# Linear attention and SwiGLU in one kernel: six of twelve token groups in natural order as four blocks of 64, decay over whole groups, one plain causal mask

## The chip, the cores and the metric

The kernel runs on one core of one Trainium2 chip. The metric is the device time of one execution in microseconds (us). All times below are of this case's runs. Each run of an experiment was timed on the same chip and in the same call as the kernel before, in alternation.

## The reference

Four sequences of 768 tokens with eight heads of 64 columns go through causal linear attention with a decay per head, in blocks of 64 tokens. The result (3072 x 512) goes through a SwiGLU FFN of width 1536.

```python
for b in range(nb):                       # blocks of 64 tokens
    intra = einsum('bhic,bhjc->bhij', qb, kb) * Dmask      # lam^(i-j), i >= j
    intra = einsum('bhij,bhjd->bhid', intra, vb)
    inter = einsum('bhid,bhde->bhie', qb * lam_pow, kv_state)
    out[:, :, sl] = intra + inter
    kv_state = lam**64 * kv_state + einsum('bhsd,bhse->bhde', kb * rev_pow, vb)
...
y = (silu(x @ w_gate) * (x @ w_val)) @ w_out               # x: attention, 3072 x 512
```

## The kernel before

Attention is done in 12 groups of 256 tokens of one sequence, FFN in 6 tiles of 512 tokens (two groups). TensorE does FFN products all the time, and the visits to attention are put between them by hand. A load gives each partition a pair of neighbouring tokens, so a row is 2 x 64 floats, 512 bytes, and k, q and v of a group are one transfer each.

```python
const = tile_pool("const", bufs=1); wpool = ...            # on-chip memory is handed out in this order
raw_pool = tile_pool("raw", bufs=10)                       # k, q, weights as loaded (f32)
...
def load_fp32(g, eng, src, what, h0=0, h1=H):              # 128 partitions x 8 heads x 512 B
    eng.dma_start(out=st[(what, g)][:, h0:h1], in_=gsrc(src, g, h0)[:, 0:h1 - h0])
...
mask = const.tile([128, 2, HP, 2, BLK], BF16, name="mask") # causal times a decay per head: 4096 B per partition
...
def scores(g, ...):                                        # 32 products of 128 columns into 4 banks
    ...
def inter(g, first):                                       # state times q: 8 full products, 128 columns
    ...
def intra(g, first):                                       # masked scores times v: 32 products of 128 columns
    ...
def attend(g):
    core(g)                                                # inter, intra, eviction
    if g + 1 < NG:
        ahead(g + 1)                                       # state update, scores of the next group
...
at(s1b[6], ahead, 4)
for _ in range(4):
    at(s1b[6], wo_cast)                                    # output weight casts on GpSimd
at(s1b[6], v_scale, 5, nc.gpsimd)
at(s1b[10], core, 4)
at(s1b[11], ffn_out, 0, 0)
at(s1b[11], ahead, 5)
```

The eight PSUM banks go round in a ring. GpSimd keeps the running state, scales v and casts weights; ScalarE evicts and casts k; VectorE masks and casts q. One queue (SP) issues the loads and the transposes, in the order of the program.

## Time and profile before

| | before |
|---|---|
| time, median of 3 | 231.78 us (231.72 to 231.91) |
| span of the profiled execution | 230.1 us |
| TensorE busy | 220.4 us, 96% |
| 512 B packets, 4 to 36 us, median | 27 ns |
| a later attention visit, inter to FFN | 1.81 us |

The chain of waits, the timelines and the hole at 68 us are shown and read in the prediction. In a timeline, a line gives the start in us, the length in us, the engine, the line of the kernel, the operation, the tile written and the tiles read, and in square brackets the engine's idle time before it and what ended that. "PEld" is the loading of weights, "SPq" and "ACTq" are issues of transfers. The packet durations come from the trace's packet records.

### The profile page before, as it was taken

What the parts mean: (1) busy time and instruction counts of PE and PEld (TensorE: products, weight loads), DVE (VectorE), ACT (ScalarE), POOL (GpSimd) and SP (SyncE); (2) the same over time, 40 slices, a digit from 0 to 9 for tenths busy, and PEclk for the clock granted to TensorE, in tenths of its full rate; (3) what the DMA queues carried; (4) which work ended last, traced back from release to release, by engine and by line L of the source; (5) the groups of instructions that cost most, each with busy time, mean ns of one, the idle gap of its engine ahead of it and who ended that gap; (6) DMA issues with size and microseconds to landing.
All of it is one profiled execution on the core that took longest, in us unless ns stands there. A gap on an engine that the chain in (4) does not pass through costs nothing.

```text
span 230.1 us, 5416 instructions
## 1 busy us (share of the span) xinstructions
PE 220.4 (96%) x2224; PEld 121.4 (53%) x2236; DVE 102.2 (44%) x187; ACT 105.1 (46%) x203; POOL 79.8 (35%) x113
## 2 busy tenths in 40 slices
PE   7899999999987999999999999999999999999994
PEld 3565456888854544464544544544544544444443
DVE  5763968675915014747273273273261223132200
ACT  6978585755532535363344363354343233322321
POOL 4476857743997703829050050050020000000000
PEclk9999999999999999999999999999999999999999
DMA  6999999899996278395918806905101101101122
GB/s 196 346 360 382 363 346 303 195 266 361 339 224 219 91 184 276 96 313 128 282 56 202 257 3 160 296 3 137 46 3 46 48 0 47 46 3 46 46 91 91
DMA packets 68906, 39.66 MB, mean 172 GB/s; under 512 B 20114, under 2 KB 64402, under 8 KB 68882
## 3 DMA queue, kind: packets, MB, share of 16 engines
q1 hardware_dynamic: 64370, 32.64, 49.6%
q10 hardware_dynamic: 4512, 6.69, 8.0%
q8 instruction: 17, 0.28, 0.5%
q14 instruction: 7, 0.06, 0.1%
HBM read 28.31 MB, written 6.29 MB: 150 GB/s over the span
## 4 chain that ended last, share of the span: by engine, by line
PE 78%; POOL 7%; DMA 6%; SPq 3%; ACT 2%; issue 2%; DVE 1%; POOLq 0%; DVEq 0%; ACTq 0%
PE bank L460 25%; PE bank L438 23%; PE bank L445 23%; DMA woraw<-in_moe_w_out_dram 3%; POOL wo_sb L212 3%; DMA qraw<-in_q_dram 2%; PE bank L401 2%; SPq L92 2%; PE bank L308 2%; PE bank L386 2%; PE bank L338 1%; POOL kvl L376 1%; POOL kvz L374 1%; POOL kvf L370 1%; POOL wv_sb L201 1%
## 5 line engine op out<-in xcount | busy, mean ns | idle before, releaser
L448 DVE TENSOR_TENSOR h<-sil,bank 128x512 bf16<-128x512 bf16 (+1 forms) x87 | 50.9, 592 | 102.5 <-PE bank L445 91.5
L438 PE MATMUL bank<-xt,wg_sb 128*128 128x512 bf16 (+1 forms) x348 | 76.6, 343 | 0.1
L445 PE MATMUL bank<-xt,wv_sb 128*128 128x512 bf16 (+1 forms) x348 | 76.5, 342 | 0.2 <-POOL wv_sb L201 0.2
L442 ACT ACTIVATE sil<-bank 128x512 bf16<-128x512 f32 (+1 forms) x87 | 45.5, 525 | 46.9 <-PE bank L438 44.5
L460 PE MATMUL bank<-wo_sb,h 128*128 128x512 bf16 (+1 forms) x288 | 64.9, 370 | 1.5 <-POOL wo_sb L212 0.8
L445 PEld LDWEIGHTS <-wv_sb 128*128 128x128 bf16 x348 | 33.9, 98 | 28.9 <-POOL wv_sb L201 1.1
L438 PEld LDWEIGHTS <-wg_sb 128*128 128x128 bf16 x348 | 32.8, 98 | 27.7 <-DVE xt L412 0.3
L460 PEld LDWEIGHTS <-h 128*128 128x128 bf16 x300 | 29.2, 98 | 33.8 <-issue 1.6
L462 ACT COPY osb<-bank 128x512 f32<-128x512 f32 (+1 forms) x24 | 13.8, 576 | 57.3 <-PE bank L460 52.5
L370 POOL TENSOR_TENSOR kvf<-kvl,ups 128x256 f32<-128x256 f32 x16 | 12.5, 782 | 64.5 <-ACT ups L360 62.9
L315 DVE TENSOR_TENSOR ssb<-bank,mask 128x512 bf16<-128x512 f32 x40 | 26.0, 683 | 8.6 <-PE bank L308 8.4
L218 POOL TENSOR_TENSOR v_s<-v,rev 128x1024 bf16<-128x1024 f32 (+1 forms) x14 | 23.1, 1655 | 8.3 <-DMA v<-in_v_dram 4.9
L412 ACT CAST xt<-bank 128x512 bf16<-128x512 f32 x21 | 14.3, 740 | 9.3 <-PE bank L401 8.3
L374 POOL CAST kvz<-kvf 64x256 bf16<-64x256 f32 x32 | 13.5, 421 | 1.7
L308 PE MATMUL bank<-qkt 64*64 64x128 bf16 x384 | 9.0, 219 | 1.2 <-DVE qkt L280 0.8
L240 DVE TENSOR_TENSOR qk<-qraw,qd 128x1024 bf16<-128x1024 f32 x8 | 10.2, 1269 | 0.0
L238 ACT CAST qk<-kraw 128x1024 bf16<-128x1024 f32 x9 | 9.4, 1042 | 0.0
L376 POOL TENSOR_TENSOR kvl<-kvf,lamblk 128x256 f32<-128x256 f32 x12 | 8.2, 683 | 1.0
L201 POOL CAST wv_sb<-wraw 128x1024 bf16<-128x1024 f32 (+1 forms) x7 | 6.5, 934 | 5.4 <-DMA wraw<-in_moe_w_val_dram 5.2
L401 PE MATMUL bank<-ssb,v_s 64*64 64x128 bf16 x384 | 8.1, 219 | 0.2 <-DVE ssb L315 0.2
L308 PEld LDWEIGHTS <-qkt 64*64 64x64 bf16 x384 | 6.6, 106 | 3.0 <-ACT qkt L272 1.8
L212 POOL CAST wo_sb<-woraw 128x1024 bf16<-128x1024 f32 x6 | 6.6, 1131 | 3.9 <-DMA woraw<-in_moe_w_out_dram 3.9
(57 smaller groups left out, 100.3 us busy)
## 6 DMA issues: line engine op xcount, KB each, us to landing
out_dram<-osb ACTq DMA_DIRECT2D x23, 256.0 KB, 2.0
kraw<-in_k_dram SPq DMA_DIRECT2D x10, 512.0 KB, 5.2
qraw<-in_q_dram SPq DMA_DIRECT2D x10, 512.0 KB, 6.2
v<-in_v_dram SPq DMA_DIRECT2D x10, 512.0 KB, 6.5
woraw<-in_moe_w_out_dram SPq DMA_DIRECT2D x6, 512.0 KB, 7.2
wraw<-in_moe_w_gate_dram SPq DMA_DIRECT2D x5, 512.0 KB, 7.0
wraw<-in_moe_w_val_dram SPq DMA_DIRECT2D x5, 512.0 KB, 7.0
kraw<-in_k_dram SPq DMA_DIRECT2D x4, 256.0 KB, 4.4
```

What stands on the lines that cost most here:

```text
L218: eng.tensor_tensor(out=st[("vs", g)][:, h0:h1], in0=st[("v", g)][:, h0:h1].rearrange("p h (s d) -> p h s d", s=2), in1=bap(rev, [[2, h1 - ...
L308: nc.tensor.matmul(sp[(c, h2)][b2 * M:b2 * M + M, n:n + BLK], tt[dp, 0, s, hp, b2 * M:b2 * M + M], tt[dp, 1, :, hp, b2 * M:b2 * M + M], st ...
L315: nc.vector.tensor_tensor(out=ssb[:, h2, 2 * c:2 * c + 2].rearrange("p a s n -> p a (s n)"), in0=sp[(c, h2)].rearrange("p (a x) -> p a x", ...
L370: nc.gpsimd.tensor_tensor(out=kv, in0=kvl[b], in1=u, op=ALU.add)
L374: nc.gpsimd.tensor_copy(out=kvz[b][(i + 1) % 2 if r else 2][dp, :, h2, :], in_=kv[dp])
L412: fns[r](out=xt[:, g % 2, :, r].rearrange("p h (m s) -> p h s m", s=2), in_=op[r].rearrange("p (h s m) -> p h s m", h=HP, s=2))
L438: nc.tensor.matmul(gp[:, 0:N], wg_sb[:, mc, fs], xt[:, b0 // 2:b1 // 2, mc].rearrange("p g b n -> p g (b n)"), start=(mc == 0), stop=(mc = ...
L442: nc.scalar.activation(sil[:, 0:N], gp[:, 0:N], AF.Silu)
L445: nc.tensor.matmul(vp[:, 0:N], wv_sb[:, mc, fs], xt[:, b0 // 2:b1 // 2, mc].rearrange("p g b n -> p g (b n)"), start=(mc == 0), stop=(mc = ...
L448: nc.vector.tensor_tensor(out=h_sb[:, fc, b0:b1].rearrange("p b n -> p (b n)"), in0=sil[:, 0:N], in1=vp[:, 0:N], op=ALU.mult)
L460: nc.tensor.matmul(ps, h_sb[:, fc, b], wo_sb[:, fc, c0:c1], start=(fc == 0), stop=(fc == FC - 1))
L462: fn(out=osb[:, c0:c1], in_=ps)
```

## The change

The intent is to take TensorE time out of the attention visits: with four blocks of 64 tokens instead of two of 128, every small product has 64 columns instead of 128. A block of 64 tokens needs tokens in natural order, one per partition, so rows are 64 floats, 256 bytes. To keep all four quadrants of the array at work, the upper 64 partitions hold head pairs exchanged; the transfers do this. The decay inside a group moves into the scales of q and v, so one causal mask serves all heads and GpSimd's state work shrinks.

```diff
+    NAT0 = 6                                   # groups 6 to 11 in natural order
...
+        if what == "v":
+            parts = [(0, 128, 0, 1, 0, H)]
+        else:
+            parts = [(0, M, 0, 1, 0, H)] + [(M, M, h2, 2, 1 - h2, HP) for h2 in range(2)]
+        for s in range(2):
+            for p0, n, d0, dh, s0_, nh in parts:
+                eng.dma_start(out=t[p0:p0 + n, ...], in_=...)   # k 6, q 6, v 2 per group
...
-    irow = const.tile([128, 2, M], FP32, name="irow")
-    irev = const.tile([128, 2], FP32, name="irev")
-    ifwd = const.tile([128, 2], FP32, name="ifwd")
-    (cinv, rev, qd, lamblk, qdec, cinvt)
-    mask = const.tile([128, 2, HP, 2, BLK], BF16, name="mask")
+    irow = const.tile([128, 2, 2, M], FP32, name="irow")
+    ipos = const.tile([128, 8], FP32, name="ipos")
+    causaln = const.tile([128, M], BF16, name="causaln")
+    (dec, qdn, lamgrp, a qdec of twice the size, two guards)
...
+    def scores_n(g):                           # 32 products of 64 columns, 2 banks
+    def guard(g):                              # one column copied by ScalarE between inter and intra
+        nc.scalar.copy(out=t, in_=st[("op", g)][1][:, 511:512])
...
     def attend(g):
-        core(g)
-        if g + 1 < NG:
-            ahead(g + 1)
+        core_a(g)                              # inter, guard
+        if g + 1 < NG:
+            upd_mm(g + 1); upd_copy(g + 1); scores(g + 1)
+        core_b(g)                              # intra, eviction
+        if g + 1 < NG:
+            state(g + 1)
...
-    for _ in range(4):
-        at(s1b[6], wo_cast)
+    at(s1b[6], wo_cast)
+    at(s1b[6], wo_cast)
     at(s1b[6], v_scale, 5, nc.gpsimd)
-    at(s1b[10], core, 4)
+    at(s1b[8], wo_cast, ACTC)                  # the fifth cast on ScalarE
+    at(s1b[8], wo_cast)
+    at(s1b[9], core_a, 4)
+    at(s1b[10], core_b, 4)
```

## The prediction

> **What bounds the kernel now.** I read the page's busy shares and the chain that ended last first, to see whether one engine sets the time.
>
> ```profile
> PE 220.4 (96%) x2224; PEld 121.4 (53%) x2236; DVE 102.2 (44%) x187; ACT 105.1 (46%) x203; POOL 79.8 (35%) x113
> ...
> PE 78%; POOL 7%; DMA 6%; SPq 3%; ACT 2%; issue 2%; DVE 1%; POOLq 0%; DVEq 0%; ACTq 0%
> ```
>
> TensorE is busy 96% of 230.1 us and carries 78% of the chain; GpSimd and DMA carry 13%. So only two things count: TensorE time in the attention blocks, and the few holes where GpSimd or DMA makes TensorE wait. The FFN (lines 438, 445, 460) isn't changed: its 864 full-width products (288 + 288 + 288 in units of 512 columns) at 0.216 us (0.86 us for four, in the chain) are 186 us.
>
> Then the timeline of TensorE, for a steady stage. Columns: start, length in us, engine, line, operation, count.
>
> ```profile
> 97.97 1.03 PE L445 MATMUL bank<-xt,wv_sb 128*128 128x512 bf16 x4
> 98.84 0.61 PE L386 MATMUL bank<-qkt,kvz 128*128 128x128 bf16 x8
> 99.38 0.64 PE L401 MATMUL bank<-ssb,v_s 64*64 64x128 bf16 x32
> 99.85 0.45 PE L338 MATMUL bank<-v_s,qk 64*64 64x64 bf16 x32
> 100.12 0.65 PE L308 MATMUL bank<-qkt 64*64 64x128 bf16 x32
> 100.84 1.02 PE L438 MATMUL bank<-xt,wg_sb 128*128 128x512 bf16 x4
> ```
>
> Ends are modelled, so I use starts. One attention visit is inter (386, the state applied to q), intra (401), the state update (338) and the next group's scores (308), with FFN work touching on both sides. 32 small products with 64 moving columns (338) take 99.85 to 100.12, **0.27 us**; 32 with 128 columns (401) take 0.47 us. That difference is what the change can earn. The later visits, without a wait, last 1.81 us (112.92 to 114.73, and three more alike).
>
> Last, the holes: the same timeline around 68 us, and GpSimd's.
>
> ```profile
> 65.69 1.98 PE L460 MATMUL bank<-wo_sb,h 128*128 128x512 bf16 x7
> 68.06 0.59 PE L460 MATMUL bank<-wo_sb,h 128*128 128x512 bf16 x2 [0.39 <-POOL wo_sb L212]
> 69.05 0.59 PE L460 MATMUL bank<-wo_sb,h 128*128 128x512 bf16 x2 [0.39 <-POOL wo_sb L212]
> 70.91 0.45 PE L338 MATMUL bank<-v_s,qk 64*64 64x64 bf16 x32 [1.27 <-POOL v_s L218]
> ```
>
> ```profile
> 65.01 3.98 POOL L212 CAST wo_sb<-woraw 128x1024 bf16<-128x1024 f32 x4
> 68.96 1.90 POOL L218 TENSOR_TENSOR v_s<-v,rev 128x1024 bf16<-128x1024 f32 x1
> ```
>
> The first output block is 12 products, 2.59 us from 65.69, so the update could begin at 68.37 after a change of tiling; it begins at 70.91. **2.5 us** are lost to GpSimd, which does four weight casts and only then scales v.
>
> **What the Trainium skill says.** "TensorE: Matmul & The Clock Gate", part 1 (Wait — 56ns, not 53.3ns?) gives N ÷ 2.4 GHz + about 2.5 ns per warm matmul, and part 3 says that products in different tiles of the array overlap. The trace agrees: 0.216 us for 512 columns; four quadrants at 128 columns would give 8 x 56 ns = 0.45 us for 32, and 0.47 is seen. With 64 columns the rule would give 0.23 and 0.27 is seen; I use 0.27. "TensorEngine Tiling (Array Packing)", Key Properties, says that changing the tiling mode drains the engine. The trace: FFN products that should end at 88.41 are followed by the update at 88.50, so about 0.09 us a change. The same page, Gotcha 1, says that different row tiles can't access one PSUM bank simultaneously. That explains the new guard: with exchanged head pairs inter and intra of one quadrant come from different row halves. "DMA: Bandwidth & Descriptors", Specifications, puts line rate at 512 B and over. No load of this kernel has 256 B rows, but its transposes move 256 B packets: in the trace's packet records they take 18 ns (median) against 27 ns for 512 B, that is 1.33 times the time per byte.
>
> **The change, part by part.**
>
> 1. Groups 6 to 11, TensorE. With four blocks of 64 tokens, scores and intra keep 32 products but with 64 columns, and inter becomes 32 products of 64 x 64 in four quadrants in place of 8 full ones. Each of the three should take the update's 0.27 us. Inter 0.54 less the change of tiling in it = 0.45, to 0.27: -0.18. Intra 0.47 to 0.27: -0.20. Scores, 88.78 to 89.33 less 0.09 = 0.46, to 0.27: -0.19. The update stays: the last groups go from 16 products in two quadrants (about 0.26, worked out from 113.93 to 114.73) to 24. Tiling changes per visit stay two. So -0.57 for each of five visits, -0.19 for group 6's early scores: **-3.0**. The wait for the eviction at 100.84 (0.16 us) should go too, since two score banks less are taken: -0.16.
>
> 2. The guard, a one-column ScalarE copy between inter and intra. Inter's issue 0.27 + a product's own length 0.19 + 0.09 to wake ScalarE (the update ends at 59.82, its copy starts at 59.91) + 0.16 for a tiny activation + 0.09 back = 0.80 us from inter's start. In five visits the update and scores (0.27 + 0.27) stand between, so intra is reached at 0.81: nothing lost. The last visit, group 11, has nothing between: 0.27 + 0.53 wait + 0.27 + two changes 0.18 = 1.25 against 1.11 (182.35 to 183.46): **+0.15**.
>
> 3. The hole at 68 us. One cast goes to ScalarE, and scaling v of group 5 comes before the last. GpSimd: the state of group 4 shrinks from 4.7 us (60.36 to 65.0) to 0.75 + 0.42 + 0.75 + 0.61 + 0.42 = about 3.0, end 63.4; two casts to 65.4, v scaled by 67.3, last cast 68.3. But ScalarE's cast needs the fifth piece of the weight, whose last packet plus the 1.65 us that the first piece took to release GpSimd gives 64.0; ScalarE, being in order, is done at 65.0 and only then does a silu (0.38) and the guard of group 4, so intra of group 4 goes at 65.65 in place of 64.23. After it: intra 0.47, one FFN column block 0.86, output block 2.59, changes 0.18: update of group 5 at about 69.8, not 70.91, **-1.1**. From there to the third tile's FFN the old time is 9.73 us (80.64); two more changes of tiling, less the 0.23 us gap before 78.27, make it about 9.8: **+0.1**.
>
> 4. Start and groups 2 and 3. Zero fills (12 x 0.27 us) and mask tables (2.9 us) leave VectorE, scaled q/k copies become one (0.84 to 0.59), the first states drop from 2.9 to 1.8 us on GpSimd. But DMA is saturated up to 36 us (345 to 385 GB/s in the windows), and v of group 2 isn't scaled before 36.6, so TensorE can't run far ahead. Group 2 loses its 0.32 us wait and gets an exposed guard of about 0.45; groups 3 and 4 get two more changes each. I call it **0**.
>
> 5. Loads of the last six groups: 14 transfers of 256 B rows per group in place of 3. Spacing of issues at the start is 0.54 us, so 7.6 us of issue; data 6144 packets / 16 x 18 ns = 6.9 us. The tightest group is 8:
>
> ```profile
> 95.16 1.55 SPq L231 DMA_TRANSPOSE qkt<-qk  x1
> 96.76 0.57 SPq L92 DMA_DIRECT2D kraw<-in_k_dram  x1
> 97.38 0.86 SPq L92 DMA_DIRECT2D qraw<-in_q_dram  x1
> 98.29 1.35 SPq L92 DMA_DIRECT2D v<-in_v_dram  x1
> 106.03 2.36 SPq L231 DMA_TRANSPOSE qkt<-qk  x1
> ```
>
> On these clocks q would land at 96.1 + 12 x 0.54 + 2 = 104.6, VectorE wants it at about 104, the transpose goes at about 106 as before and takes 4.4 us, and its reader comes at 114. It is hidden, with about 3 us to spare. **0**.
>
> Sum: -3.0 - 0.16 + 0.15 - 1.1 + 0.1 = -4.0. 231.78 - 4.0 = 227.8 us; I say 227.7, 1.8% less.
>
> **Rivals.** *Loads become the bound.* For it: the rows are half as long, the queue is in order, and a transpose waits behind 14 issues; if each issue took 1 us, q of group 8 would land near 110 and its transpose at 115, a stall of 2 us, 229.5 us or so. Against it: issues of 256 rows take 0.47 us, and after 75 us the DMA share is 0.6. *ScalarE becomes the wait.* It takes guards and wider update copies (0.58 in place of 0.33) ahead of evictions, so the eviction ends about 2.85 us after inter starts and the next tile's FFN wants it at 2.94. If I am off by 0.4, two tile borders stall, +0.8 together. *GpSimd becomes the wait:* a state of four blocks is about 6.1 us of GpSimd in groups 6 and 7, but visits are 10 us or more apart; against it, and worth 1 us at most. *The small products don't shrink* (if their issue costs more than the update's 8.4 ns each): part 1 halves, 229.3 us. *The hole closes wholly:* if the weight lands sooner, part 3 gives 1.1 us more, 226.6.
>
> **Range and chances.** Parts 1 and 3 each have about 1 us of error, parts 4 and 5 mostly on the slow side. 226.2 to 229.4. A 2% gain needs 227.1 or less, 0.6 under my number: 0.34. Slower by 2% would need two rivals at once: 0.03.
>
> **What would show it.** In the changed profile: visits of groups 6 to 10 of about 1.25 us from inter to FFN; inter, intra and scores 0.27 us from start to start; no idle before intra except in groups 2 and 11 (0.5 us); the update of group 5 at 69 to 70 us; no wait of ScalarE or VectorE for k or q after 80 us; GpSimd idle before each state. It is wrong if TensorE waits for a transpose, an eviction or a guard in those visits, or if the hole at 68 us is as wide as before.

## The result, and the profile after

The changed kernel is correct and slower: **240.24 us** (median of 4, 237.77 to 242.73), against 231.84 us for the kernel before in the same rounds. The ratio is 1.032, with a 95% interval of 1.022 to 1.042. A ratio here is the mean time of one kernel's fast runs over that of the other's fast runs in the same rounds, so it isn't quite the ratio of the medians.

Two lines of the changed kernel's page, busy times and the chain that ended last:

```profile
PE 223.1 (93%) x2432; PEld 119.9 (50%) x2444; DVE 90.2 (38%) x154; ACT 107.2 (45%) x209; POOL 84.9 (35%) x130
...
PE 74%; DMA 15%; SPq 3%; issue 2%; POOL 2%; ACT 2%; DVE 1%; ACTq 0%; POOLq 0%
```

TensorE's share falls to 93% of a longer span, and DMA's part of the chain rises from 6% to 15%. GpSimd's falls from 7% to 2%: the holes that the change aimed at were replaced by waits for transfers. To see where, I compared start times in both timelines:

| us | before | after | shift |
|---|---|---|---|
| first FFN gate | 15.40 | 17.49 | +2.1 |
| update of group 4 | 59.37 | 63.81 | +4.4 |
| update of group 5 (after the hole) | 70.91 | 75.83 | +4.9 |
| third tile's FFN | 80.64 | 85.85 | +5.2 |
| visit of group 6 | 98.84 | 103.98 | +5.1 |
| visit of group 8 | 130.28 | 140.93 | +10.65 |
| visit of group 11 | 182.35 | 191.74 | +9.4 |

The time is lost in two places: 4.4 us before 60 us, and 5.5 us between the visits of groups 6 and 8. After that it comes back at 0.35 to 0.5 us a visit, as intended.

*The start.* The same stretch of both kernels, first the kernel before, then the changed one. Columns: stretch, its length, then busy time and instructions of TensorE, its weight loads, VectorE, ScalarE and GpSimd, then the granted TensorE clock, the DMA share and GB/s.

```profile
4.00:8.00 4.00, 3.26 (x40) 1.85 (x38) 1.98 (x7) 3.82 (x14) 1.06 (x2) 1.00 1.15 345
```

```profile
4.00:8.00 4.00, 3.58 (x36) 2.26 (x35) 1.63 (x5) 3.47 (x9) 0.76 (x2) 1.00 1.16 292
```

The DMA engines are as busy as before, but move 292 GB/s instead of 345. In the packet records a 512 B packet takes 31 to 32 ns, not 27. The transfers here are those of the kernel before, byte for byte; the change touches only groups from the seventh on.

*Group 8.* The changed kernel's TensorE at the visit of group 7, which also does the update and the scores of group 8:

```profile
121.76 0.44 PE L385 MATMUL bank<-v_s,qk 64*64 64x64 bf16 x24 [2.37 <-POOL v_s L243]
122.93 0.45 PE L357 MATMUL bank<-qkt 64*64 64x64 bf16 x32 [0.74 <-DMA qkt<-qk]
...
123.60 1.68 PE L519 MATMUL bank<-xt,wg_sb 128*128 128x512 bf16 x4
```

The update waits for scaled v, the scores for the transpose. Behind the first wait is a load:

```profile
119.79 1.91 POOL L243 TENSOR_TENSOR v_s<-v,dec 128x1024 bf16<-128x1024 f32 x1 [7.72 <-DMA v<-in_v_dram]
```

And behind the load is the queue, which issues the 14 transfers of group 8 between two transposes:

```profile
103.73 5.07 SPq L110 DMA_DIRECT2D kraw<-in_k_dram  x6
108.84 4.96 SPq L110 DMA_DIRECT2D qraw<-in_q_dram  x6
113.85 1.44 SPq L110 DMA_DIRECT2D v<-in_v_dram  x2
117.66 2.38 SPq L256 DMA_TRANSPOSE qkt<-qk  x1
```

The queue needs from 103.73 to 115.29, 11.6 us, for what took 2.9 us before. That is 0.84 us for each of the twelve of k and q (103.73 to 113.85), against the 0.54 that I had taken. In the trace's records of single issues, ten of the fourteen hold the queue for 0.60 to 0.64 us, the other four for 0.79 to 1.65, and the gaps between them are under 0.05 us. So at this place it is the issues themselves that take the time, and not waits of the queue between them; why four take longer isn't known. After the wait the FFN products are slow: four take 1.47, then 1.71, then 1.11 us (from start to start) instead of 0.86, and the granted clock of 124 to 128 us is 0.59. This costs another 1.7 us. "TensorE: Matmul & The Clock Gate", part 1, of the Trainium skill says that the clock falls to half after an idle window of about 3.4 us. Here TensorE waited 3.1 us in two pieces (2.37 and 0.74), with 24 short products in between: the half clock follows the wait, but no piece was as long as that window.

*The hole.* ScalarE and then TensorE in the changed kernel, with the guard of group 4:

```profile
70.26 1.04 ACT L237 CAST wo_sb<-woraw 128x1024 bf16<-128x1024 f32 x1 [3.73 <-DMA woraw<-in_moe_w_out_dram]
...
71.49 0.15 ACT L448 COPY guard<-bank 128x1 f32<-128x1 f32 x1
```

```profile
71.69 0.64 PE L477 MATMUL bank<-ssb,v_s 64*64 64x128 bf16 x32 [1.59 <-ACT guard L448]
```

The wait for GpSimd is gone, but ScalarE stands 3.73 us before a weight that hasn't landed, and the guard and intra stand behind it. So the hole is +0.5 us, where I had expected -1.1.

### The profile page after: what moved, and what is told of

The parts are those of the page before. It is cut to its first block, busy times and chain, and to the rows that moved or that the text cites. A ratio compares the mean times of both kernels' runs of the same rounds, so it can differ in the third digit from the quotient of the medians.

```text
span 239.6 us, 5923 instructions
## 1 busy us (share of the span) xinstructions
PE 223.1 (93%) x2432; PEld 119.9 (50%) x2444; DVE 90.2 (38%) x154; ACT 107.2 (45%) x209; POOL 84.9 (35%) x130
## 4 chain that ended last, share of the span: by engine, by line
PE 74%; DMA 15%; SPq 3%; issue 2%; POOL 2%; ACT 2%; DVE 1%; ACTq 0%; POOLq 0%
PE bank L541 25%; PE bank L519 20%; PE bank L526 19%; DMA woraw<-in_moe_w_out_dram 4%; DMA wraw<-in_moe_w_val_dram 4%; DMA v<-in_v_dram 3%; DMA qkt<-qk 2%; PE bank L477 2%; DMA kraw<-in_k_dram 1%; PE bank L385 1%; PE bank L464 1%; SPq L232 1%; SPq L100 1%; PE bank L171 1%; PE bank L331 1%
## 5 line engine op out<-in xcount | busy, mean ns | idle before, releaser
L243 POOL TENSOR_TENSOR v_s<-v,dec 128x1024 bf16<-128x1024 f32 (+1 forms) x14 | 23.2, 1666 | 36.0 <-DMA v<-in_v_dram 25.4
L424 POOL TENSOR_TENSOR kvf<-kvs,ups 128x256 f32<-128x256 f32 x8 | 5.8, 724 | 33.3 <-ACT ups L407 26.1
L338 DVE TENSOR_TENSOR ssb<-bank,causal 128x512 bf16<-128x512 f32 x24 | 15.5, 684 | 3.6 <-PE bank L331 3.5
L265 DVE TENSOR_TENSOR qk<-qraw,qdn 128x1024 bf16<-128x1024 f32 x6 | 7.5, 1245 | 15.2 <-DMA qraw<-in_q_dram 15.2
L407 ACT COPY ups<-bank 128x256 f32<-128x256 f32 (+1 forms) x24 | 9.5, 448 | 5.7 <-PE bank L385 4.1
L424 POOL TENSOR_TENSOR kvf<-kvf,ups 128x256 f32<-128x256 f32 x16 | 11.6, 724 | 0.6
L362 DVE TENSOR_TENSOR ssb<-bank,causaln 128x512 bf16<-128x512 f32 x12 | 8.3, 688 | 6.1 <-PE bank L357 6.0
L433 POOL CAST kvn<-kvf 64x256 bf16<-64x256 f32 x24 | 9.5, 394 | 1.5
L477 PE MATMUL bank<-ssb,v_s 64*64 64x128 bf16 (+1 forms) x384 | 7.1, 207 | 2.3 <-ACT guard L448 2.1
L385 PE MATMUL bank<-v_s,qk 64*64 64x64 bf16 x352 | 5.5, 198 | 3.2 <-POOL v_s L243 3.2
```

The costliest lines, as they stand in the source:

```text
L243: eng.tensor_tensor(out=st[("vs", g)][:, h0:h1], in0=st[("v", g)][:, h0:h1].rearrange("p h (s d) -> p h s d", s=2), in1=vfac(g, h0, h1), o ...
L338: nc.vector.tensor_tensor(out=ssb[:, h2, 2 * c:2 * c + 2].rearrange("p a s n -> p a (s n)"), in0=sp[(c, h2)].rearrange("p (a x) -> p a x", ...
L407: nc.scalar.copy(out=u[:, 0:n], in_=up[r][:, 0:n])
L424: nc.gpsimd.tensor_tensor(out=o, in0=f, in1=u, op=ALU.add)
L477: nc.tensor.matmul(op[r][h2 * 64:h2 * 64 + 64, cols(g, hp, s)], v_s[ps, 2 * hp + h2, s], ssb[ps, h2, hp * 2 + s] if g >= NAT0 else ssb[ps, ...
```

## The experiments

The first question was whether the slow packets belong to the kernel or to the moment; the second, whether the 14 transfers cost by their number or by their short rows.

### ctl_before and ctl_after: both kernels again, on one chip

No edit.

> The kernel before again, profiled on the chip on which the next three run. Two theories of the late start (first FFN gate at 17.5 us in the changed kernel, 15.4 us before, with 512 B packets at 31-32 ns against 27 ns). If the changed kernel's own order causes it, this run shows 27 ns and 15.4 us again. If it is the chip or the moment, it shows about 31 ns and 17 us, and its time is about 2 us above 231.8.

> The changed kernel again: 237.5 to 240.5 us, about 3.2% over the kernel before; the transfers of group 8 again issued at about 0.84 us each, the half-clock stretch at 124 us again if it follows from the wait for group 8 and not from chance. If the late start was the moment only, it is 2 to 4 us shorter.

Measured: 232.47 us (20 runs) and 240.62 us (4 runs), ratio of the latter to before 1.034 (1.028 to 1.041). The stretches from 4 to 8 us, kernel before, then changed kernel:

```profile
4.00:8.00 4.00, 3.77 (x40) 2.17 (x38) 1.71 (x6) 3.55 (x13) 0.81 (x1) 1.00 1.12 336
```

```profile
4.00:8.00 4.00, 3.16 (x40) 1.82 (x38) 1.79 (x5) 3.59 (x10) 0.74 (x2) 1.00 1.17 293
```

The median packet takes 27 ns and 32 ns again, on the same chip. So it is the kernel and not the moment. The half clock came again in the changed kernel, this time after group 7's wait (0.50 from 108 to 110 us); the kernel before had one as well, after its own hole (0.50 from 72 to 74 us). Its 20 runs lie between 231.54 and 233.64 us.

### loads_512x3 and loads_512x14: few transfers, and as many with long rows

```diff
-        if g < NAT0:
+        if True:                               # loads_512x3: groups 6 to 11 as before; result wrong on purpose
             eng.dma_start(out=t[:, h0:h1], in_=gsrc(src, g, h0)[:, 0:h1 - h0])
```

```diff
-            parts = ...                        # loads_512x14: same 14 shares of bytes, 512 B rows; wrong on purpose
+            parts = [(0, 128, 4 * s, 4)] if what == "v" else \
+                    [(0, M, 4 * s, 4)] + [(M, M, 4 * s + 2 * x, 2) for x in range(2)]
```

> The changed kernel with groups 6 to 11 loaded as before, in 3 transfers of 512 B rows (the result is wrong on purpose: tokens lie in the wrong order). Theory that the 14 transfers per group are the loss: no wait for q, k, v or a transpose after 80 us, visits of groups 7 to 10 about 1.3 us, no half clock; the shift against before falls from about +9 us to about +2 (start +4.4 and hole +0.5 less 6 x 0.5 for the visits), so 233 to 235 us. Rival, GpSimd's four-block states or ScalarE's guards and wider copies hold TensorE after 80 us: 238 to 240 us as in the changed kernel.

> The changed kernel with groups 6 to 11 in 14 transfers as the change has them, of the same bytes each, but in 512 B rows, half the packets (wrong result on purpose). If the count of transfers is the cost (issue spacing 0.84 us whatever the rows): 238 to 240 us, like the changed kernel, group 8's fourteen issues again some 11.5 us. If the 256 B packets are the cost: like the run with 3 transfers, 233 to 235 us, and issues of 0.5 us.

Measured: 235.61 us with 3 transfers (0.6 over the upper end of what I had expected), **245.52 us** with 14 transfers of long rows. The two differ only in how the same rows are split into transfers, so the splitting is a cost; the short row is not, since half the packets made it no faster. That it was slower than the changed kernel by 5 us I had not expected. ScalarE in that run shows a further wait:

```profile
79.61 0.36 ACTq L539 DMA_DIRECT2D out_dram<-osb  x1
80.09 0.65 ACT L402 COPY ups<-bank 128x256 f32<-128x256 f32 x2 [4.00 <-DMA qraw<-in_q_dram]
```

ScalarE has nothing to do with q; it was held 4.00 us at the store of an output. In the built program all hardware transfers, stores too, take one of eight semaphores in turn and wait for the transfer eight before. With 14 loads to a group that is often a load. The copy that stood behind it feeds the state of group 5, and the output products of that stage come 4.0 us later than in the changed kernel (87.47 against 83.47). Why it hit this run harder than the changed kernel, whose ScalarE lost 1.88 us there, isn't settled.

But 3 transfers leave 3.2 us over the kernel before, and the shift at the update of group 4 is still +4.4. The start is a separate matter.

### align256, align64 and before_off32: where the buffers lie

In the built program's tile addresses the weights began at byte 24,832 of each partition before the change and at 22,560 after. 24,832 is 97 x 256; 22,560 is 88 x 256 + 32. All later tiles have sizes that are multiples of 256, so before the change every one of these buffers began at a multiple of 256 bytes, and after it every one 32 bytes past one. The cause is the sum of the constants ahead of them: with sizes rounded up to 32 bytes 8,320 before and 6,048 after, each on top of 16,512.

"DMA: Bandwidth & Descriptors", How a descriptor splits into AXI transactions, of the Trainium skill, says that a transaction must start at an address that is a multiple of 256 bytes, so that a descriptor that doesn't start at one begins with a transaction from the boundary below. Worked out by this rule, an estimate: a row of 512 bytes that begins 32 bytes past a boundary takes three transactions and not two. The page words the rule for reads, and here the buffer on the chip is written. It made the offset worth a test: an unused tile of 224 bytes, or of 32.

```diff
+    const.tile([128, 56], FP32, name="pad")    # align256, in the changed kernel; align64: [128, 8]
     wg_sb = wpool.tile([128, MC, DFF], BF16, name="wg_sb")
```

```diff
+    const.tile([128, 8], FP32, name="pad")     # before_off32, in the kernel before
     wg_sb = wpool.tile([128, MC, DFF], BF16, name="wg_sb")
```

> The changed kernel with one unused tile of 224 bytes per partition ahead of the weights, so that every buffer a transfer writes starts at a multiple of 256 bytes in its partition, as it did before the change (in the changed kernel the smaller constants leave all of them at 32 bytes past one). Nothing else differs. Theory that this offset slows the transfers: 512 B packets at 27 ns instead of 31-32, first FFN gate at 15.4-15.9 us instead of 17.5, shift at the second tile 0 to +1 us instead of +4.4, total 235.5 to 237 us. Rival, the changed order of work at the start slows the transfers: packets stay at 31 ns, 240.5 us.

> The same with 32 bytes in place of 224: buffers start at a multiple of 64 but not of 256 bytes (64 past one). If what counts is 64 bytes: like the run at 256, 235.5 to 237 us and 27 ns. If what counts is 256 bytes, or the rows straddle it: 31 ns and 240.5 us as in the changed kernel.

> The kernel before with an unused tile of 32 bytes ahead of the weights and nothing else: all its buffers 32 bytes past a multiple of 256. Theory of the offset: 512 B packets at 31 ns, first gate at about 17.3 us, total 234.5 to 236.5 us, 1 to 2% slower, with no other part of the change. Rival: the same as before, 231.8 to 232.5 us.

Measured: align256 **232.34 us** (20 runs, 228.21 to 236.95), align64 240.15 us, before_off32 **239.53 us**. An unused tile of 32 bytes, and nothing else, makes the kernel before 3.0% slower (2.4 to 3.6%), nearly as much as the whole change did. 224 bytes take some 8 us from the changed kernel. A multiple of 64 doesn't help; 256 does. The direction was as expected each time, the size was not: I had expected 235.5 to 237 us for align256 and 234.5 to 236.5 us for before_off32, so the offset costs some 3 to 4 us more than I thought. In before_off32, the stretch from 4 to 8 us and TensorE at the old hole:

```profile
4.00:8.00 4.00, 3.15 (x40) 1.85 (x38) 1.74 (x5) 3.49 (x13) 0.39 (x1) 1.00 1.17 292
```

```profile
71.76 0.59 PE L461 MATMUL bank<-wo_sb,h 128*128 128x512 bf16 x2 [1.25 <-POOL wo_sb L213]
```

In align256, the same stretch is back at the rate of the kernel before:

```profile
4.00:8.00 4.00, 3.77 (x38) 2.47 (x37) 1.75 (x6) 3.36 (x9) 1.35 (x3) 1.00 1.15 345
```

before_off32 has 292 GB/s again, and its hole is deeper, since the weights land later: the update of group 5 is at 76.57, 5.7 us later than in the kernel before. About 3 us of this are there at the update of group 4 (62.42 against 59.37). After the hole its granted clock is 0.50 from 74 to 80 us. The packet records, medians in ns:

| bytes, stretch | ctl_before | before_off32 | ctl_after | align64 | align256 |
|---|---|---|---|---|---|
| 512, 4-36 us | 27 | 32 | 32 | 32 | 27 |
| 1024, 4-36 us | 46 | 51 | 51 | 51 | 46 |
| 256, after 75 us | 18 | 18 | 18 | 18 | 18 |

The median is about 5 ns higher, whether for 512 or for 1024 bytes. But this isn't a fixed price of every packet. In ctl_before 99% of the 512 B packets of this stretch take 27 ns; in before_off32 16% still do, and the rest spread up to 38 ns (90th percentile) and beyond. After 75 us, where the DMA engines are less busy, the median of its 512 B packets is 29 ns, and in loads_512x14, with the same offset, 94% of them take at most 27 ns. If each row paid for one more transaction, these would be slow too; whether the offset costs time only where many engines write at once, or only in transfers of a certain shape, no run here separates. The packets of 256 B show no difference in the median, where the page's rule would give two transactions and not one. Their means are 18.3 ns in align256 and 19.4 in ctl_after, so the loads of groups 6 to 11 themselves hardly suffer. In before_off32 these packets are the transposes alone, and their mean is 23.4 ns against 19.2 in ctl_before.

align256 still waits for group 8:

```profile
113.03 0.44 PE L386 MATMUL bank<-v_s,qk 64*64 64x64 bf16 x24 [0.85 <-POOL v_s L244]
115.45 0.64 PE L358 MATMUL bank<-qkt 64*64 64x64 bf16 x32 [1.98 <-DMA qkt<-qk]
```

This profile is of a run counted as slow (233.22 us), and only 9 of its 20 runs count as fast. The ratio of the fast ones, 0.9905, therefore flatters it; the median is 0.4 us above that of the kernel before. In the profile the granted clock is 0.89 from 112 to 128 us after these waits, and I think that the spread comes from that, but didn't test it.

### align256_512x3: both causes taken away

Both edits together (result wrong on purpose).

> The changed kernel with both suspected losses taken away: buffers at multiples of 256 bytes, and groups 6 to 11 in 3 transfers of 512 B rows (wrong result on purpose). If the two are all that the prediction missed besides the hole at 68 us (which came out +0.5 and not -1.1): 229 to 230.5 us. If they hide each other's cost (the first stall gives the loads more time): 231 to 233 us.

Measured: **228.18 us**, ratio 0.982 (0.976 to 0.988), 3.8 us under the kernel before; a little better than expected. The prediction was 227.7. The queue has time to spare, and no visit waits for a transfer:

```profile
106.04 0.52 SPq L100 DMA_DIRECT2D kraw<-in_k_dram  x1
106.66 0.52 SPq L100 DMA_DIRECT2D qraw<-in_q_dram  x1
107.27 1.29 SPq L100 DMA_DIRECT2D v<-in_v_dram  x1
```

With three other runs this makes a square of medians (two of them were timed on another chip, where the kernel before took 0.5 us longer): 240.6 (offset, 14 transfers), 235.6 (offset, 3), 232.3 (aligned, 14), 228.2 (aligned, 3). The offset costs 7.4 to 8.3 us and the transfers 4.2 to 5.0; they add up nearly.

### align256_6dma and align256_qact: correct versions with fewer issues on the queue

```diff
-            parts = [(0, M, 0, 1, 0, H)] + [(M, M, h2, 2, 1 - h2, HP) for h2 in range(2)]
+            parts = [(0, 128, 0, 1, 0, H)]     # align256_6dma: 2 transfers for each of k, q, v
...
+            nc.scalar.copy(out=ko[lo], in_=ki[lo])
+            for x in range(2):                 # the casts exchange the heads of the upper tokens (q alike)
+                nc.scalar.copy(out=ko[hi, x:H:2], in_=ki[hi, 1 - x:H:2])
```

```diff
-                load_fp32(g, nc.sync, src, what)
+                load_fp32(g, nc.scalar if what == "qraw" and g >= NAT0 else nc.sync, src, what)   # align256_qact
```

> A candidate for the better version, with a correct result: buffers at multiples of 256 bytes, groups 6 to 11 in 6 transfers of 256 B rows instead of 14; the head pairs of the upper tokens are exchanged by the casts instead (3 instructions on ScalarE for k and 3 on VectorE for q, in place of one each). Theory that the count of issues is what the loads cost: 6 x 0.84 = 5 us of issue per group instead of 11.5, no wait of TensorE for a transpose or for v after 80 us, 228 to 229.5 us, close to the 228.2 of the run with 3 transfers. Rival, the longer casts (about +1.2 us on both engines per group) make ScalarE or VectorE the wait: 230 to 232 us.

> Buffers at multiples of 256 bytes, 14 transfers per group as in the change, but the six of q issued by ScalarE, the eight of k and v by the other queue. Result correct. If the one queue's rate of issue is the cost: 8 x 0.84 = 6.7 us there, q lands some 5 us earlier, 228.5 to 230.5 us. Rival: the issues hold ScalarE (0.34 us each, more where it waits for a buffer or for the transfer eight before), evictions and silus come late: 232 us or more.

Measured: align256_6dma **229.04 us**, ratio 0.987 (0.983 to 0.990), correct, and faster than both kernels (the gain is under 2%, but the interval lies wholly below 1). Its rows are 256 B as in the change, so the row isn't what cost the time. Of the waits for transfers, one of 0.55 us for scaled v of group 7 is left. align256_qact took 251.95 us. One line of its ScalarE:

```profile
60.52 10.85 ACTq L110 DMA_DIRECT2D qraw<-in_q_dram  x5
```

The rival of that run was right, and by far more than I had allowed: five issues held ScalarE for 10.85 us. The trace's records of single issues divide this time: the five issues themselves took 0.60 to 0.65 us each, 3.1 us together, and 7.7 us were waits between them. In the program these issues wait for the semaphore that they then use, so for the transfer eight before, and not for a free buffer.

### align256_nat12: no group in four blocks

```diff
-    NAT0 = 6
+    NAT0 = 12
```

> Buffers at multiples of 256 bytes, and no group in four blocks: all twelve keep pairs of tokens and 512 B rows; the rest of the change (state, masks, order, guard) stays. Result correct. The prediction gave the four blocks 3.0 us; if so this run is 3 us over the 228.2 of the aligned run with 3 transfers: 230.7 to 231.7 us, visits of 1.8 us or more. If they are worth half: 229.7 us.

Measured: 236.86 us, 8.7 over the aligned run with 3 transfers (on another chip), where I had expected 3. It doesn't isolate what I wanted, so the worth of the four blocks rests on the start times and not on this run. TensorE at the visit of group 7:

```profile
114.78 0.63 PE L478 MATMUL bank<-ssb,v_s 64*64 64x128 bf16 x32
116.24 1.02 PE L520 MATMUL bank<-xt,wg_sb 128*128 128x512 bf16 x4 [0.83 <-ACT xt L490]
```

The new order puts intra last. With two-block scores a visit takes 2 + 2 + 4 = 8 banks, the whole ring, so the next FFN product needs a bank that intra has just written and waits for its eviction: 0.83 us, and the visit lasts 2.63 us (113.61 to 116.24), not 1.81. With four blocks it takes 2 + 2 + 2 banks and doesn't wait; in the aligned run with 3 transfers a visit lasts 1.23 us (127.50 to 128.73). So the new order is good only together with the four blocks.

### align256_6dma_oldhole and best_dve: the order at the hole

```diff
-    at(s1b[8], wo_cast, ACTC)                  # oldhole: four casts on GpSimd, then v_scale, as before the change
+    at(s1b[8], wo_cast, DVEC)                  # best_dve: the fifth cast on VectorE
```

> The run with 6 transfers, but the last output weight cast back on GpSimd and the scaling of v of group 5 behind all four casts, as before the change. The prediction gave the new order -1.1 us; the aligned runs reach the update of group 5 at 69.0-69.4 us, 70.9 before. Expected 1.1 to 1.9 us over the run with 6 transfers, with waits for the weight casts back at 68 us. Rival, the smaller state alone made room on GpSimd: within 0.4 us of it.

> The version with aligned buffers and 6 transfers, with one more step: the fifth output weight is cast by VectorE instead of ScalarE, so that the guard of group 4 doesn't stand behind it. Expected: the 1.17 us wait of group 4's intra at 66.1 us goes, the update of group 5 at 69.0-69.3 us, total 227.8 to 228.9 us, 0 to 1 us under the run with 6 transfers. Rival: VectorE, in order, holds up the FFN products while it waits for the weight, same time.

Measured: 228.68 us and 228.93 us, both within the scatter of align256_6dma (229.04; ratios to before 0.986 and 0.985, with intervals that overlap its own). The rival was right: the new order gives nothing. First TensorE of align256_6dma, then of the old order:

```profile
66.10 0.64 PE L485 MATMUL bank<-ssb,v_s 64*64 64x128 bf16 x32 [1.17 <-ACT guard L456]
```

```profile
69.51 0.44 PE L393 MATMUL bank<-v_s,qk 64*64 64x64 bf16 x32 [0.54 <-POOL v_s L244]
```

In the one the guard waits behind ScalarE's weight cast, in the other the update waits a little for GpSimd. The old order's update of group 5 is at 69.51, against 70.91 in the kernel before. So moving the casts isn't what gains at the hole. What is left of the change there is GpSimd's smaller state (group 4's takes 3.0 us, 60.63 to 63.59, in place of 4.7), and the earlier inter and guard; no run takes the state alone, so that it is the state is an inference. With the cast on VectorE the 1.17 us wait does go, but one of 0.40 us for a weight cast on GpSimd comes, and the total doesn't show it.

### align_loadbufs and off_loadbufs: which buffers

Unused tiles between the pools put the load buffers (k, q, weights and v as loaded) at multiples of 256 and all else 32 bytes past, and the reverse.

> The changed kernel with only the load buffers (k, q, weights and v as they come from memory) moved to multiples of 256 bytes; weights in use, transposed and all other tiles stay 32 bytes past one. If the rows that loads write are what the offset slows: 512 B packets at 27 ns, total as with all buffers aligned, 229 to 235 us. If the transposes or the engines' own tiles carry it: 238 to 241 us.

> The reverse: all tiles at multiples of 256 bytes except the load buffers, which stay 32 bytes past one. Load theory: 512 B packets at 31-32 ns, 238 to 241 us as in the changed kernel. If transposes or engine tiles carry it: 229 to 235 us.

Measured: 235.06 us (232.76 to 238.32) and 238.5 us (236.3 to 240.18). The stretch from 4 to 8 us of each, in this order:

```profile
4.00:8.00 4.00, 3.59 (x40) 2.09 (x38) 1.79 (x6) 3.55 (x10) 1.35 (x3) 1.00 1.15 344
```

```profile
4.00:8.00 4.00, 3.52 (x36) 2.17 (x35) 1.60 (x5) 3.40 (x9) 0.77 (x2) 1.00 1.17 294
```

The slow packets go with the load buffers: a median of 27 ns in the first, 32 ns in the second. Four runs of each scatter by 4 to 6 us, the second profile is of a slow run, and the first kernel has only two fast runs and no interval, so whether the offset of the other tiles (the transposes' above all) costs a further 2 us is left open.

All runs, medians in us, with the ratio to the kernel before of the same rounds:

| run | offset, bytes | transfers per group 6 to 11 | us | before | ratio (95%) |
|---|---|---|---|---|---|
| ctl_before | 0 | 3 | 232.47 | 232.43 | 1.000 (0.998-1.002) |
| before_off32 | 32 | 3 | 239.53 | 231.96 | 1.030 (1.024-1.036) |
| ctl_after | 32 | 14 | 240.62 | 232.43 | 1.034 (1.028-1.041) |
| align64 | 64 | 14 | 240.15 | 231.96 | 1.032 (1.025-1.039) |
| align256 | 0 | 14 | 232.34 | 231.96 | 0.991 (0.987-0.994), 9 fast of 20 |
| loads_512x3 (wrong) | 32 | 3 | 235.61 | 232.43 | 1.015 (1.009-1.020) |
| loads_512x14 (wrong) | 32 | 14 | 245.52 | 232.43 | 1.058 (1.052-1.064) |
| align256_512x3 (wrong) | 0 | 3 | 228.18 | 231.96 | 0.982 (0.976-0.988) |
| align256_6dma | 0 | 6 | 229.04 | 231.89 | 0.987 (0.983-0.990) |
| align256_6dma_oldhole | 0 | 6 | 228.68 | 231.89 | 0.986 (0.983-0.989) |
| best_dve | 0 | 6 | 228.93 | 232.50 | 0.985 (0.981-0.989) |
| align256_nat12 | 0 | 3 | 236.86 | 231.89 | 1.020 (1.017-1.023) |
| align256_qact | 0 | 14 | 251.95 | 231.89 | 1.084 (1.080-1.089) |
| align_loadbufs | loads 0, rest 32 | 14 | 235.06 | 232.50 | none |
| off_loadbufs | loads 32, rest 0 | 14 | 238.50 | 232.50 | 1.021 (1.015-1.027) |

## Why the prediction was wrong

The prediction was 227.7 us in a range of 226.2 to 229.4; 240.24 came. Two of its steps failed, the start and the loads of the last groups, both of which it had set to 0. Its terms can be read off the start times (shifts against the kernel before, of the profiled executions, all three in the fast state):

| term of the sum | predicted | changed kernel | aligned, 6 transfers | aligned, 3 transfers |
|---|---|---|---|---|
| start, to the update of group 4 | 0 | +4.4 | +0.4 | +0.1 |
| hole, to the update of group 5 | -1.1 | +0.5 | -1.0 | -2.0 |
| to the third tile's FFN | +0.1 | +0.3 | +0.2 | +0.2 |
| groups 6 to 11, to the last visit | -3.0 - 0.16 | +4.2 | -1.9 | -2.6 |
| last visit | +0.15 | 0 | 0 | 0 |

- **Part 4, start: "I call it 0". This step failed.** It took the transfer rate of the kernel before ("345 to 385 GB/s"; the window from 32 to 36 us has 339) over to the changed kernel. The prediction counted the mask table as work that goes away, but not that it was also bytes in front of every load buffer. With the constants changed, the buffers began 32 bytes past a multiple of 256, the median 512 B packet took 32 ns instead of 27, and +4.4 us came in place of 0. Aligned, the term is +0.1 to +0.4, so the step was right about all that it had looked at.
- **Part 5, loads: "hidden, with about 3 us to spare". This step failed as well.** The term was the spacing of issues: 0.54 us taken from the first 4 us of the kernel, 0.84 us measured for group 8, so 11.6 us of issue and not 7.6. The trace of the kernel before already had a larger spacing a little later, 0.74 us:

```profile
8.45 0.69 SPq L193 DMA_DIRECT2D wraw<-in_moe_w_gate_dram  x1
9.19 0.69 SPq L193 DMA_DIRECT2D wraw<-in_moe_w_val_dram  x1
9.92 0.69 SPq L193 DMA_DIRECT2D wraw<-in_moe_w_gate_dram  x1
```

Nor did the argument against the rival hold, "issues of 256 rows take 0.47 us": those of 256 rows of 256 B took 0.63 us (medians of k and of q) in the changed kernel. I had named the rival, "if each issue took 1 us", with a stall of 2 us. That was the right mechanism. The waits at group 8 are 2.37 + 0.74 us, the scores of group 7 wait 1.22 (the profile names a ScalarE copy, but their transpose lands at 106.04 us and they start at 106.08), and the half clock afterwards costs 1.7 us more; the rival had left out what a stall does to the clock.
- **Part 3, hole: right in size only without the offset, and for another reason.** That ScalarE would stand before the fifth weight, with the guard behind it, was predicted; that slow packets would bring its cast to 70.26 us (64.67 in the aligned run with 6 transfers) was not. Aligned, with 6 transfers, group 4's intra is at 66.10 (65.65 predicted), and the update of group 5 is reached 1.0 us earlier relative to the start. But the old order does as well (its update is at 69.51), so the size of the term came out by luck, as far as the moved cast is concerned.
- **Part 1, TensorE: right, but a sixth too large.** Visits of groups 8, 9 and 10 last 1.31, 1.38 and 1.19 us in the changed kernel and those of 7 to 9 last 1.23 to 1.24 us in the aligned run with 3 transfers, 1.25 predicted; they were 1.81. From the third tile to the last visit the aligned run gains 2.6 us where 3.16 was said. That is because the count from inter to FFN leaves out something: the four FFN products before inter now take 0.96 us to the start of inter (143.42 to 144.38), where they took 0.86. This agrees with a change of tiling that now stands before inter. So a visit gains about 0.48 us and not 0.57. The rival that the small products don't shrink fell.
- **Part 2, guard: right for the later visits.** Where the update and scores stand between, no wait for it is seen in the aligned runs. The last visit came out at 0 and not +0.15.

With both causes gone the sum is -3.8 us by the medians (228.18 against 231.96), and -4.0 was the prediction. Part of this agreement is luck: the hole gained more than predicted, and the visits less. So what failed was not, in the main, the accounting of TensorE but the assumption that transfers that the change doesn't touch stay as they were.

**The better version** is the changed kernel with 224 unused bytes ahead of the weights and 6 transfers per group: 229.04 us, 1.3% faster than the kernel before (0.983 to 0.990) and correct; its two variants at the hole are within the scatter.

## What to carry to other kernels

Whenever a change adds or removes on-chip constants, look at where the load buffers begin afterwards; here 32 bytes of offset cost 3%, and the sign that gives it away is a median packet that takes 5 ns longer in a stretch with the DMA busy throughout. Count transfers, not only bytes: an in-order queue that issues 14 small transfers ahead of a transpose delays that transpose, and stores and loads that share a few semaphores make an engine wait for transfers it has nothing to do with. Predict a wait together with what it does to the clock afterwards.

## What the Trainium skill lacked or had wrong

- "DMA: Bandwidth & Descriptors", How a descriptor splits into AXI transactions: it gives the 256 B rule with beats, but not the price for buffers on the chip. The runs show a median that is 5 ns higher while the DMA is busy (512 B 27 to 32 ns, 1024 B 46 to 51 ns, none for 256 B), a rate of 292 in place of 345 GB/s, and 3.0% of a whole kernel for 32 bytes of offset (before_off32). Its Rules for kernel authors have no line on where a buffer should begin.
- "Collectives: The Full Stack", Rules for kernel authors, asks for buffers aligned to 32 bytes, there for collectives. For plain loads here buffers 32 or 64 bytes past a multiple of 256 were slow (240.62 and 240.15 us), those at a multiple of 256 were not (232.34).
- "DMA: Bandwidth & Descriptors", Issuing engines are not separate DMA queues, calls the time to initiate a transfer usually small relative to the transfer. Here the issue of 64 KB held the queue for 0.63 us and that of 128 KB for 0.61 to 0.62 us (medians in the changed kernel), no less than the shortest issues of 512 KB of k, q and v in the kernel before (0.52 to 0.57 us); 14 of them took 11.6 us. No page says what issues cost that wait for the transfer eight before, where a program shares eight semaphores; ScalarE lost 4.00 us in loads_512x14 and 7.7 us in align256_qact to it.
- "TensorE: Matmul & The Clock Gate", part 1, ties the half clock to an idle window of about 3.4 us. In ctl_after it followed a wait of 1.78 us in one piece, with TensorE busy for 0.24 us of 104 to 106 us: no idle window of that length was needed. The same part's second failure mode, short idle pieces between groups of products, is nearer to this, but gives no length.
